# Attention and a four-expert layer on one core: the first second-layer weights summed on another engine, and sums and operands formed at other places

## The chip, the core and the metric

The kernel runs on one core of a Trainium2 chip. The metric is device time in microseconds, the median of several executions; lower is better. TensorE (PE) multiplies matrices, VectorE (DVE), ScalarE (ACT) and GpSimd (POOL) work on tiles, and SyncE (SP) issues the DMA transfers. Each engine takes its instructions in the order in which the program issues them.

## The reference

Attention with a cumulative bias over 32 heads, and then, for each of 2304 tokens, a sum over four experts of two matrix products with a ReLU between them:

```python
attn = softmax(q @ k.T / sqrt(D) + bias)      # 4 x 8 heads, 576 rows, D = 64
x = attn @ v                                  # laid out as 2304 x 512
p = domain_probs / (domain_probs.sum(-1, keepdims=True) + 1e-09)
for e in range(4):
    h = np.maximum(x @ w1[e], 0.0)            # w1[e]: 512 x 1024
    out += p[:, e:e + 1] * (h @ w2[e])        # w2[e]: 1024 x 512
```

## The kernel before

**Stages.** A planner written in the kernel (class Sched) orders the attention, and with it the beginning of expert 0. What remains of expert 0 is emitted by the loop from line 1209 on: a first and a second layer for each group of tokens. Experts 1 to 3 follow in a form of their own, in which the order is written out by hand. The change touches the end of expert 0 and that last part.

**Precision.** Each matrix operand is split in two: a rounded part (hi, on ACT, line 457) and the residue (sub, line 444, mostly on DVE), so a product takes three matmuls per block.

**Items and products.** Experts 1 to 3 are cut into 18 work items: half of an expert's hidden width by a third of the tokens, in the order expert, half, third. Each item has a first and a second layer, and each layer is computed with seven block products in place of eight, on sums of blocks (a Strassen form). One product is twelve matmuls of 128x128 by 128x384: six into each of two PSUM banks (product, line 1262). The program issues the first layer of item 0, then, for each item, the first layer of the next item and after it the second layer of this one.

**Banks.** bA, bB, bC and bM are pairs of PSUM banks. In both layers seven products go to these in the order 1, 6, 5, 7, 2, 4, 3 (first layer, line 1284) and 1, 6, 2, 5, 7, 3, 4 (second layer, line 1382). pass_on (line 1273, "the hand-over") copies one pair into another on ACT: bA to bC after product 1 of the first layer, bC to bB after products 1 and 7 of the second. Product 6 continues in the pair just copied, so it waits for the copy.

**First layer.** keep (line 1297) copies a pair of banks to SBUF on ACT: c12 after product 6, c22 after product 7, in item 0 also c11 and h21. plus (line 1305) adds another pair to it on DVE (line 1307) and then gates it: ReLU times the token's probability (line 1278). c11 is complete after product 2, h21 after product 4, c12 after product 3.

**Second-layer operands.** From c11, c12, c22 and h21 DVE forms s5 = c22 + h21, s7 = c11 - h21, s6 = c11 - s5 and s3 = c12 + s6 (add, line 1055). operand (line 1350) splits c11, c12, c22, s5, s6, s7 and s3 into operands 1, 2, 4, 5, 6, 7 and 3; the residues of 7 and 3 are POOL's, that of 5 is POOL's except in item 0. The tables START, FIRST, EARLY, REST, ALL and LAST (lines 41 to 46) say after which product which of these steps is issued. START belongs to the first layer of item 0. FIRST belongs to the first layer of item 1 and forms operands of item 0. EARLY belongs to the second layers of items 0 to 15 and forms those of the item after; REST belongs to the first layers behind these.

**Second layer.** update (line 1384) adds a pair of banks to acc in SBUF on DVE (line 1390): bC after product 6, bB after 2, bM after 5, bC after 7, bM after 3, bB after 4. Product 3 continues in bM and waits for the update after product 5.

**Weights.** w_steps (line 1125) returns a list: sums (line 1132), which forms sums of the four staged weight blocks, and seven calls of split (line 1145) for the seven weights. side is a list from which both layers take such steps, two after each product in the first layer of item 0. wsteps is its like at the end of expert 0: from the last first-layer group on, the loop takes up to three steps after each group of a layer. Temporary tiles t come from a pool of six; x operands from a pool of seven, each loaded when the product before it in that buffer is done.

The names in the trace have their buffer numbers left out: pb are the banks of bA, bB and bC, mo those of bM, hT_r, xg and hx the operands (hx is operand 3), osb the gate weights.

Of the kernel before, what the change touches and what calls it, by code (L numbers as in the profile page):

```python
# [11 lines left out]
F32 = mybir.dt.float32  # L12
F32R = mybir.dt.float32r
AF = mybir.ActivationFunctionType
ALU = mybir.AluOpType
# [8 lines left out]
P = 128  # L24
NC = 5
TG = 384
# [11 lines left out]
HALVES = [(e, s) for e in range(1, E) for s in range(2)]  # L38
T_PREP = (10.0, 28.0, 47.0)
T_LOAD = 6.0  # L40
START = {7: "4", 4: "1", 3: "s5 s7"}
EARLY = {1: "1", 6: "s5", 2: "2 s7", 5: "s6", 4: "4"}
REST = {1: "6 5", 6: "s3 7", 5: "3"}
ALL = {4: "4", 1: "1", 2: "2", 6: "6", 5: "5", 7: "7", 3: "s3 3"}
LAST = {4: "s5 s7", 3: "s6"}
FIRST = {1: "2 5 s6", 6: "6", 5: "s3 7", 7: "3"}
PRODUCTS = (1, 6, 5, 7, 2, 4, 3)


def rows(m):  # L50
    return (0, 64) if m == 0 else (128 * m - 64, 128 * m + 64)


def t_pe(n):
    return max(n / 2.4 + 13.5, 110)
# [271 lines left out]
def body(ctx, tc, qk, qkv0, vp, s, dp, w1, w1s, w2, w2s, out):  # L327
# [23 lines left out]
    def slot(name, shape, dt, pool=hpool):  # L351

        if late.get(name, (None, None))[0] != dt:
            late[name] = (dt, pool.tile(shape, dt, tag=name, name=f"{name}_{'r' if dt == F32R else 'f'}"))
        return late[name][1]

    def hT(l):
        return slot(f"hT{l}", [P, KF, TG], F32R)
# [84 lines left out]
    def sub(e, out, in0, in1):  # L443
        (nc.gpsimd if e == "POOL" else nc.vector).tensor_tensor(out=out, in0=in0, in1=in1, op=ALU.subtract)  # L444
# [10 lines left out]
    def hi(e, out, in_):  # L455
        if e == "ACT":
            nc.scalar.activation(out, in_, AF.Copy)  # L457
        elif e == "POOL":
            nc.gpsimd.tensor_scalar(out, in_, 1.0, 1.0, op0=ALU.mult, op1=ALU.mult)
        else:  # L460
            nc.vector.tensor_copy(out, in_)
# [183 lines left out]
    for j, (h, ms) in enumerate(VISITS):  # L645
        base = 1000.0 * (j + 1)
        b, hh = divmod(h, NH)
        o = 64 * (hh % 2)
# [71 lines left out]
        for m in ms[1:] if joint else ms:  # L720
            pr = base + PM * m
            a, bb = rows(m)
            n = bb - a
# [181 lines left out]
    for which in (1, 2):  # L905
        for i in range(4):
# [3 lines left out]
            n, lo = 1024 // WH, None  # L910
# [13 lines left out]
    def load_x(tiles, dc):  # L924
        n0, w = tiles[0] * P, len(tiles) * P
        nc.sync.dma_start(out=xgt[:, :, dc, 0:w].bitcast(F32), in_=xw[dc // 2, dc % 2, :, :, n0:n0 + w])
# [3 lines left out]
    def l1_mm(fc, w, t, u0, u1):  # L930
        recent[0] = t
        q, o = fc // 2, 128 * (fc % 2)
        for u in range(u0, u1):
            dc, part = divmod(u, 3)
            wl, l = ((w1h, 0), (w1h, 1), (w1l, 0))[part]
            nc.tensor.matmul(t[:, 0:w], wl[q][:, dc, o:o + P], xgt[:, l, dc, 0:w], start=(u == 0), stop=(u == 3 * KD - 1))  # L936

    def l1_hi(fc, w, t):
        nc.scalar.activation(hT(0)[:, fc, 0:w], t[:, 0:w], AF.Relu)

    def l1_lo(fc, w, t):
        nc.vector.scalar_tensor_tensor(out=hT(1)[:, fc, 0:w], in0=t[:, 0:w], scalar=0.0, in1=hT(0)[:, fc, 0:w].bitcast(F32),
                                       op0=ALU.max, op1=ALU.subtract)
# [70 lines left out]
    mpool = ctx.enter_context(tc.tile_pool(name="moe", bufs=1))  # L1014
    xpool = ctx.enter_context(tc.tile_pool(name="xring", bufs=7))
    tpool = ctx.enter_context(tc.tile_pool(name="temps", bufs=6))
    spool = ctx.enter_context(tc.tile_pool(name="stage", bufs=1))
# [17 lines left out]
    def temp():  # L1035
        return tpool.tile([P, 2, TG], F32, tag="t", name="t")
# [17 lines left out]
    def add(e, out, in0, in1, op):  # L1054
        (nc.gpsimd if e == "POOL" else nc.vector).tensor_tensor(out=out, in0=in0, in1=in1, op=op)  # L1055
# [69 lines left out]
    def w_steps(which, begin=False):  # L1125

        b = stage.pop(which)
        neg = which == 2
        part = w1_part if which == 1 else w2_part
        src = {1: b[0, 0], 2: b[1, 0], 3: b[1, 1], 7: b[0, 1], 4: b[1, 0]}  # L1130

        def sums():
            if begin:
                src[5], src[6], src[4] = (t.rearrange("p a b -> p (a b)") for t in (spool.tile([P, 1, 512], F32, tag="t2", name="t2"), temp(), temp()))
                src[5], src[6], src[4] = (t[:, 0:512] for t in (src[5], src[6], src[4]))
                add("POOL", src[5], b[0, 1], b[0, 0], ALU.subtract)
                add("POOL", src[7], b[1, 1], b[0, 1], ALU.subtract)
                add("POOL", src[6], b[1, 1], src[5], ALU.subtract)
                add("POOL", src[4], b[1, 0], src[6], ALU.subtract)
                return  # L1140
            src[5] = src[6] = spool.tile([P, 1, 512], F32, tag="t2", name="t2")[:, 0]
            add("POOL", src[5], b[0, 1], b[0, 0], ALU.subtract)
            add("POOL", src[7], b[1, 1], b[0, 1], ALU.subtract)

        def split(o, e):
            hi("ACT", part(o, 0), src[o])
            sub(e, part(o, 1), src[o], part(o, 0).bitcast(F32))
            if begin:
                pass
            elif o == 5 and neg:  # L1150
                add("POOL", src[6], src[5], b[1, 1], ALU.subtract)
            elif o == 5:
                add("POOL", src[6], b[1, 1], src[5], ALU.subtract)
            if o == (6 if neg else 2) and not begin:
                add("POOL", src[4], src[4], src[6], ALU.add if neg else ALU.subtract)

        return [sums] + [lambda o=o, e=e: split(o, e) for o, e in (
            tuple((o, "DVE") for o in PRODUCTS) if begin else
            ((5, "POOL"), (1, "POOL"), (2, "POOL"), (6, "POOL"), (4, "POOL"), (7, "DVE"), (3, "DVE")) if which == 1 else
            ((1, "DVE"), (2, "DVE"), (5, "DVE"), (6, "DVE"), (7, "POOL"), (3, "DVE"), (4, "DVE")))]  # L1160

# [7 lines left out]
    def bank(k):  # L1169
        if k in tok:  # L1170
            return tok[k]
        if k not in cur:
            b = nbuf[0] % len(banks)
            cur[k] = 1 - b if b < 2 and banks[b] is recent[0] else b
            nbuf[0] += 1
        return banks[cur[k]]
# [22 lines left out]
    w1_first = []  # L1199
# [8 lines left out]
    wsteps = []  # L1208
    for i, x in enumerate(prog):
        if x[0] == "load":  # L1210
            if x[2].done is None:
                load_x(x[1], x[3])
        elif x[0] == "l1":
            if x[4].done is None:
                l1_mm(x[1], x[2], bank(x[5]), x[3], x[3] + UN)
                spent += UN * t_pe(x[2]) / 1e3
        elif x[0] == "l1e":
            if x[3].done is None:
                l1_hi(x[1], x[2], bank(x[5]))
            if x[4].done is None:  # L1220
                l1_lo(x[1], x[2], bank(x[5]))
        elif x[0] == "l2":
            if x[3].done is None:
                l2_mm(x[1], x[5], bank(x[4]), x[2], x[2] + UN)
                spent += UN * t_pe(x[5]) / 1e3
        else:
            gi, dt = x[1]
            n0, n1 = GROUPS0[gi][0] * P, GROUPS0[gi][-1] * P + P
            if x[2].done is None:
                evict0(gi, dt, bank(x[4]))  # L1230
            else:
                if x[3].done is None:
                    nc.sync.dma_start(out=o_d[dt * P:(dt + 1) * P, n0:n1], in_=tok["osb", x[1]][:, 0:n1 - n0])
                spilled.append((dt, n0, n1))
        if x[0] in ("l1", "l2"):
            while steps and steps[0][0] <= spent:
                steps.pop(0)[3]()
        if i == last_l1:
            wsteps = w1_first
        if i >= last_l1 and wsteps and x[0] in ("l1e", "l2e"):  # L1240
            for _ in range(3):
                if wsteps:
                    wsteps.pop(0)()
# [5 lines left out]
        for b_, u0, u1 in blocks_of(n0, n1):  # L1249
            nc.sync.dma_start(out=acc[dt][b_][:, u0 - TG * b_:u1 - TG * b_], in_=o_d[dt * P:(dt + 1) * P, u0:u1])  # L1250
    bA, bB, bC, bM = ([t[:, 0:TG] for t in ts] for ts in (pb[0:2], pb[2:4], pb[4:6], mo))
    hx = mpool.tile([P, 2, 2, TG], F32R, name="hx")

    def h_part(o, l):
        if o == 3:
            return hx[:, l]
        if o in (6, 7):
            return xgt[:, l, 2 * (o - 6):2 * (o - 6) + 2, :]
        n = (1, 2, 4, 5).index(o)
        return hT(l)[:, 2 * n:2 * n + 2, :]  # L1260
# [21 lines left out]
    side = []  # L1282
# [143 lines left out]
    def next_probs(w_i):  # L1426
        if w_i < len(work):
            n, g = work[w_i]
            load_prob(HALVES[n][0], NP * g, osb2)

    next_probs(0)
    side.extend(w_steps(2))
    tmp = {}
    steps = operands(tmp, e5="DVE")
    first_layer(0, plan(steps, START), tmp)
    next_probs(1)
    for w_i, (n, g) in enumerate(work):
        more = n + 1 < len(HALVES)
        if w_i + 1 < len(work):
# [8 lines left out]
            tmp = {}  # L1448
            at = plan(steps, REST if w_i else FIRST)
            steps = operands(tmp, True, last=w_i + 2 == len(work))  # L1450
# [7 lines left out]
        if g == 2 and more:  # L1458
            w2_next = w_steps(2)
            side.extend(w2_next[:4])  # L1460
            del w2_next[:4]
        second_layer(w_i, n, g, plan(steps, EARLY if w_i + 2 < len(work) else ALL if w_i + 2 == len(work) else {}))
        while side:
# [33 lines left out]
```

## Time and profile before

| | us |
|---|---|
| median of 3 runs | 928.04 (928.01 to 928.5) |
| profiled execution | 928.9 |
| its span | 927.1 |

| engine | busy us | share of the span |
|---|---|---|
| PE | 914.6 | 99% |
| DVE | 676.2 | 73% |
| ACT | 480.0 | 52% |
| POOL | 498.5 | 54% |

The span runs from the first to the last instruction in the profile; the rest of the profiled execution lies around it. Busy time counts an instruction from its start to its end, and matmuls overlap their neighbours. Bracketed times in the timeline are the idle time of that engine just before the row, with the engine, tile and line that released it. x2 means that two like instructions in a row are drawn as one.

### The profile page before, as it was taken

How to read it: one execution, taken by the hardware profiler on the slowest of the kernel's cores; microseconds unless marked ns; L12 is line 12 of the kernel's file. 1: busy time of each engine (PE TensorE's matmuls, PEld its weight loads, DVE VectorE, ACT ScalarE, POOL GpSimd, SP SyncE). 2: the span in 40 equal slices, each digit the busy share in tenths (PEclk: the TensorE clock that was granted, in tenths of full speed). 3: DMA queues.
4: the chain of work that ended last, by engine and by line, in shares of the span. 5: the costliest groups of instructions: out<-in, count | busy, mean ns of one | idle time of the engine just before them, and what ended most of it. 6: DMA issues, size and time to landing. Idle time of an engine off the chain costs nothing.

```text
span 927.1 us, 16473 instructions
## 1 busy us (share of the span) xinstructions
PE 914.6 (99%) x5590; PEld 884.6 (95%) x5590; DVE 676.2 (73%) x1568; ACT 480.0 (52%) x1094; POOL 498.5 (54%) x530
## 2 busy tenths in 40 slices
PE   9999999999999999999999999999999999999998
PEld 6789999899999999988999999999999999999998
DVE  6878788887861121588878787878777878688885
ACT  6898999898960110342444334435343534344342
POOL 4688888787733699120754174536444624471322
PEclk9999999999999999999999999999999999999999
DMA  6788878869526984597775658665786468744703
GB/s 167 188 250 253 225 215 228 239 185 256 168 78 217 327 292 160 164 309 258 255 244 190 217 207 300 207 203 175 273 272 205 160 221 301 243 158 157 269 27 119
DMA packets 131039, 198.85 MB, mean 214 GB/s; under 512 B 11448, under 2 KB 107772, under 8 KB 130956
## 3 DMA queue, kind: packets, MB, share of 16 engines
q1 hardware_dynamic: 130956, 197.81, 66.7%
q8 instruction: 44, 0.72, 0.3%
q14 instruction: 39, 0.32, 0.1%
HBM read 154.85 MB, written 29.05 MB: 198 GB/s over the span
## 4 chain that ended last, share of the span: by engine, by line
PE 84%; DVE 8%; ACT 4%; issue 2%; POOL 1%; DMA 0%; SPq 0%; ACTq 0%; POOLq 0%
PE pb L1267 43%; PE mo L1267 7%; PE mo L950 7%; PE mo L936 6%; PE pv L835 4%; PE pb L936 4%; PE pb L950 3%; PE T L785 3%; PE S L739 3%; PE S L736 1%; DVE acc L1390 1%; DVE hT_r L444 1%; DVE t L1055 1%; PE X L785 1%; ACT a L758 1%
## 5 line engine op out<-in xcount | busy, mean ns | idle before, releaser
L1267 PE MATMUL pb<-x,w1h 128*128 128x384 f32 x1008 | 256.9, 335 | 2.9 <-ACT pb L1275 1.6
L1267 PEld LDWEIGHTS pb<-x,w1h 128*128 128x128 f32 x1008 | 181.0, 188 | 5.9 <-ACT t L1300 2.2
L1267 PE MATMUL pb<-x,w1l 128*128 128x384 f32 x504 | 168.5, 334 | 0.0
L1275 ACT ACTIVATE pb<-pb 128x384 f32<-128x384 f32 x106 | 50.1, 474 | 162.5 <-DVE t L1307 99.5
L444 POOL TENSOR_TENSOR hT_r<-t,hT_r 128x768 fp32r<-128x768 f32 x17 | 31.8, 1873 | 178.6 <-PE pb L1267 143.5
L457 ACT ACTIVATE hT_r<-t 128x768 fp32r<-128x768 f32 x72 | 60.8, 845 | 103.2 <-PE pb L1267 95.1
L1267 PE MATMUL pb<-hT_r,w2h 128*128 128x384 f32 x432 | 109.7, 334 | 0.8 <-DVE t L1278 0.8
L1267 PEld LDWEIGHTS pb<-x,w1l 128*128 128x128 f32 x504 | 94.6, 188 | 0.0
L758 ACT ACTIVATE a<-a,mx 128x576 f32<-128x576 f32 (+4 forms) x136 | 81.0, 597 | 13.3 <-DVE mx L750 10.1
L1390 DVE TENSOR_TENSOR acc<-pb,acc 128x384 f32<-128x384 f32 x144 | 74.7, 551 | 12.4 <-PE pb L1267 9.5
L1267 PEld LDWEIGHTS pb<-hT_r,w2h 128*128 128x128 f32 x432 | 77.9, 188 | 1.1 <-DVE t L1278 1.1
L936 PE MATMUL mo<-xg,w1h 128*128 128x384 f32 (+1 forms) x304 | 78.3, 327 | 0.0
L452 POOL TENSOR_SCALAR a<-a,sm 128x576 f32<-128x576 f32 (+5 forms) x111 | 60.9, 555 | 28.6 <-DVE sm L766 15.0
L444 DVE TENSOR_TENSOR hT_r<-t,hT_r 128x768 fp32r<-128x768 f32 x55 | 57.6, 1049 | 24.0 <-ACT hT_r L457 23.5
L1267 PE MATMUL pb<-xg,w2h 128*128 128x384 f32 x288 | 73.4, 335 | 0.5 <-ACT pb L1275 0.5
L1267 PE MATMUL pb<-hT_r,w2l 128*128 128x384 f32 x216 | 72.2, 334 | 0.0
L1055 DVE TENSOR_TENSOR t<-t 128x768 f32<-128x768 f32 (+1 forms) x40 | 65.0, 1632 | 0.0
L1307 DVE TENSOR_TENSOR t<-pb,t 128x384 f32<-128x384 f32 x74 | 37.8, 552 | 34.6 <-ACT t L1300 22.4
L950 PE MATMUL mo<-hT_r,w2h 128*128 128x256 f32 (+1 forms) x320 | 58.3, 314 | 0.0
L814 DVE TENSOR_TENSOR aTl<-T,aTh 128x256 fp32r<-128x256 f32 (+2 forms) x103 | 51.2, 508 | 4.9 <-ACT aTh L457 3.7
L750 DVE CUSTOM_DVE_ANT_0 a<-S,mask 128x448 f32<-128x448 f32 (+4 forms) x107 | 48.2, 456 | 8.7 <-PE S L736 6.1
L936 PEld LDWEIGHTS mo<-xg,w1h 128*128 128x128 f32 x304 | 52.1, 190 | 1.4 <-issue 0.7
(217 smaller groups left out, 2310.3 us busy)
## 6 DMA issues: line engine op xcount, KB each, us to landing
x<-xs_d SPq DMA_DIRECT2D x68, 768.0 KB
x<-x_d SPq DMA_DIRECT2D x55, 768.0 KB
xs_d<-x SPq DMA_DIRECT2D x12, 768.0 KB
KK<-AB_r SPq DMA_DIRECT2D x24, 288.0 KB
osb<-p_d SPq DMA_DIRECT2D x18, 384.0 KB
xg<-x_d SPq DMA_DIRECT2D x16, 384.0 KB
w1r<-in_w1s_dram SPq DMA_DIRECT2D x6, 1024.0 KB
w2r<-in_w2s_dram SPq DMA_DIRECT2D x6, 1024.0 KB
```

The lines of the kernel that those rows point to most:

```text
L444: (nc.gpsimd if e == "POOL" else nc.vector).tensor_tensor(out=out, in0=in0, in1=in1, op=ALU.subtract)
L452: (nc.gpsimd if e == "POOL" else nc.vector).tensor_scalar(out, in_, scale, 1.0 if bias is None else bias, op0=ALU.mult, op1=ALU.mult if bi ...
L457: nc.scalar.activation(out, in_, AF.Copy)
L750: nc.vector.tensor_tensor_reduce(out=z[0:n, j0:j1], in0=tok["S", (c, pi)][0:n, 0:j1 - j0], in1=mask[0:n, 448 - a + j0:448 - a + j1], scale ...
L758: nc.scalar.activation(z[0:n, 0:bb], z[0:n, 0:bb], AF.Exp, bias=tok["mx", c][0:n, k:k + 1], scale=-1.0, accum_out=tok["sm", c][0:n])
L814: nc.vector.tensor_tensor(out=dst, in0=src, in1=h_.bitcast(F32), op=ALU.subtract)
L936: nc.tensor.matmul(t[:, 0:w], wl[q][:, dc, o:o + P], xgt[:, l, dc, 0:w], start=(u == 0), stop=(u == 3 * KD - 1))
L950: nc.tensor.matmul(t[:, 0:w], wl[fc // 2][:, fc % 2, 128 * dt:128 * dt + 128], ht[:, fc, 0:w], start=(u == 0), stop=(u == 3 * KF - 1))
L1055: (nc.gpsimd if e == "POOL" else nc.vector).tensor_tensor(out=out, in0=in0, in1=in1, op=op)
L1267: nc.tensor.matmul(ts[u], wv[wl][:, k, 128 * u:128 * u + 128], x[xl_][:, k, :], start=start and k == 0 and n == 0, stop=k == 1 and n == 2, ...
L1275: nc.scalar.activation(out[u], in_[u], AF.Copy)
L1390: nc.vector.tensor_tensor(out=d, in0=ts[u], in1=d, op=ALU.add)
```

## The change

The tables START, EARLY and FIRST change. With START and FIRST, s5, s7 and operand 1 of item 0 are formed after product 1 of the next first layer, s6 and operand 6 after product 6, operand 2 and s3 after product 5, operand 5 after product 4, operands 7 and 3 after product 3. With EARLY, s7 follows product 5, operand 2 follows product 7 and s6 follows product 3.

The weights of the first second layer are summed in one step of four subtractions and additions on DVE, as was done for the first-layer weights on POOL, and not with two on POOL at first and two between the splits. This step is issued at the end of expert 0. The sums lie in the memory of hx, which operand 3 takes over later, and the seven residues are all DVE's, in the order 1, 6, 2, 5, 7, 3, 4.

```diff
-START = {7: "4", 4: "1", 3: "s5 s7"}
-EARLY = {1: "1", 6: "s5", 2: "2 s7", 5: "s6", 4: "4"}
+START = {7: "4"}
+EARLY = {1: "1", 6: "s5", 5: "s7", 7: "2", 3: "s6", 4: "4"}
-FIRST = {1: "2 5 s6", 6: "6", 5: "s3 7", 7: "3"}
+FIRST = {1: "s5 s7 1", 6: "s6 6", 5: "2 s3", 4: "5", 3: "7 3"}
...
             if begin:
-                src[5], src[6], src[4] = (t.rearrange("p a b -> p (a b)") for t in (spool.tile([P, 1, 512], F32, tag="t2", name="t2"), temp(), temp()))
-                src[5], src[6], src[4] = (t[:, 0:512] for t in (src[5], src[6], src[4]))
-                add("POOL", src[5], b[0, 1], b[0, 0], ALU.subtract)
-                add("POOL", src[7], b[1, 1], b[0, 1], ALU.subtract)
-                add("POOL", src[6], b[1, 1], src[5], ALU.subtract)
-                add("POOL", src[4], b[1, 0], src[6], ALU.subtract)
+                if which == 1:
+                    ts = (spool.tile([P, 1, 512], F32, tag="t2", name="t2"), temp(), temp())
+                    src[5], src[6], src[4] = (t.rearrange("p a b -> p (a b)")[:, 0:512] for t in ts)
+                else:
+                    t = slot("hx", [P, 2, 2, TG], F32, mpool).rearrange("p a b n -> p (a b n)")
+                    src[5], src[6], src[4] = (t[:, 512 * i:512 * i + 512] for i in range(3))
+                e = "DVE" if neg else "POOL"
+                add(e, src[5], b[0, 1], b[0, 0], ALU.subtract)
+                add(e, src[7], b[1, 1], b[0, 1], ALU.subtract)
+                add(e, src[6], *((src[5], b[1, 1]) if neg else (b[1, 1], src[5])), ALU.subtract)
+                add(e, src[4], b[1, 0], src[6], ALU.add if neg else ALU.subtract)
                 return
...
-            tuple((o, "DVE") for o in PRODUCTS) if begin else
+            tuple((o, "DVE") for o in (PRODUCTS if which == 1 else (1, 6, 2, 5, 7, 3, 4))) if begin else
...
         if i == last_l1:
-            wsteps = w1_first
+            w2_first = w_steps(2, True)
+            wsteps = w1_first + w2_first[0:1]
...
-    hx = mpool.tile([P, 2, 2, TG], F32R, name="hx")
-
     def h_part(o, l):
         if o == 3:
-            return hx[:, l]
+            return slot("hx", [P, 2, 2, TG], F32R, mpool)[:, l]
...
-    side.extend(w_steps(2))
+    side.extend(w2_first[1:])
```

## Rows read from the trace of the kernel before

**Rows 1.** The page's head: the span, and busy time of each engine.
```profile
span 927.1 us, 16473 instructions
...
PE 914.6 (99%) x5590; PEld 884.6 (95%) x5590; DVE 676.2 (73%) x1568; ACT 480.0 (52%) x1094; POOL 498.5 (54%) x530
```

**Rows 2.** Busy us by stretch: length, PE, weight loads, DVE, ACT, POOL, clock, DMA.
```profile
387.60:436.50 48.90, 44.66 (x252) 42.92 (x251) 38.48 (x56) 18.72 (x34) 8.01 (x5) 1.00 0.85 293
436.50:525.00 88.50, 88.26 (x506) 87.24 (x506) 70.86 (x105) 37.29 (x65) 41.19 (x23) 1.00 0.66 225
```

**Rows 3.** Timeline of PE: start, length, operation, count, idle time before and releaser.
```profile
387.61 0.52 PE L1267 MATMUL pb<-x,w1h 128*128 128x384 f32 x2
...
404.10 0.34 PE L1267 MATMUL pb<-x,w1l 128*128 128x384 f32 x1
406.04 0.61 PE L1267 MATMUL pb<-x,w1h 128*128 128x384 f32 x2 [1.60 <-ACT pb L1275]
...
424.42 0.62 PE L1267 MATMUL pb<-xg,w2h 128*128 128x384 f32 x2 [0.54 <-ACT pb L1275]
...
462.13 0.61 PE L1267 MATMUL mo<-hx,w2h 128*128 128x384 f32 x2
...
491.81 0.62 PE L1267 MATMUL mo<-hx,w2h 128*128 128x384 f32 x2 [0.24 <-DVE acc L1390]
...
550.60 0.61 PE L1267 MATMUL mo<-hx,w2h 128*128 128x384 f32 x2
```

**Rows 4.** Waits of the weight loads from 376 on: total us, times, longest us.
```profile
PEld mo L1267 <- DVE acc L1390: 4.4, 10, 0.6
...
PEld pb L1267 <- ACT t L1300: 2.2, 6, 0.7
```

**Rows 5.** Timeline of ACT, 395 to 425.
```profile
395.71 0.64 ACT L457 ACTIVATE w2h<-t 128x512 fp32r<-128x512 f32 x1 [2.21 <-POOL t L1055]
...
396.77 0.86 ACT L1300 ACTIVATE t<-pb 128x384 f32<-128x384 f32 x2
...
404.77 0.84 ACT L457 ACTIVATE hT_r<-t 128x768 fp32r<-128x768 f32 x1 [2.35 <-DVE t L1278]
405.52 0.85 ACT L1275 ACTIVATE pb<-pb 128x384 f32<-128x384 f32 x2
...
423.89 0.86 ACT L1275 ACTIVATE pb<-pb 128x384 f32<-128x384 f32 x2 [5.60 <-PE pb L1267]
```

**Rows 6.** Timeline of DVE, 390 to 462.
```profile
390.94 0.69 DVE L444 TENSOR_TENSOR w2l<-w2r,w2h 128x512 fp32r<-128x512 f32 x1 [2.70 <-ACT w2h L457]
...
397.66 1.02 DVE L1307 TENSOR_TENSOR t<-pb,t 128x384 f32<-128x384 f32 x2
...
408.45 1.96 DVE L1055 TENSOR_TENSOR t<-t 128x384 f32<-128x384 f32 x4
410.32 1.82 DVE L444 TENSOR_TENSOR hT_r<-t,hT_r 128x768 fp32r<-128x768 f32 x2
412.06 0.95 DVE L1055 TENSOR_TENSOR t<-t 128x768 f32<-128x768 f32 x1
...
418.38 2.63 DVE L1278 SCALAR_TENSOR_TENSOR t<-t,osb 128x768 f32<-128x768 f32 x1
...
447.11 2.07 DVE L1278 SCALAR_TENSOR_TENSOR t<-t,osb 128x768 f32<-128x768 f32 x1
...
458.89 1.78 DVE L444 TENSOR_TENSOR hT_r<-t,hT_r 128x768 fp32r<-128x768 f32 x1
460.60 1.00 DVE L1055 TENSOR_TENSOR t<-t,pb 128x384 f32<-128x384 f32 x2
461.53 1.01 DVE L1390 TENSOR_TENSOR acc<-mo,acc 128x384 f32<-128x384 f32 x2
```

**Rows 7.** Timeline of POOL: residues of operand 3.
```profile
418.37 1.83 POOL L444 TENSOR_TENSOR hx<-t,hx 128x768 fp32r<-128x768 f32 x1 [1.77 <-ACT hx L457]
...
448.32 2.57 POOL L444 TENSOR_TENSOR hx<-t,hx 128x768 fp32r<-128x768 f32 x1
```

## The prediction, made before the change was run

> **What bounds the kernel now.** I read the page's head first: PE is busy 914.6 of 927.1 us [rows 1]. So almost all of the time is matmuls, and this change removes none of them: it can only win back PE's idle time. The busy time by stretch says where that is: 4.24 us between 387.6 and 436.5, and about 0.25 in each later stretch of three items [rows 2]. "Idle" is too small a figure, because matmuls overlap; their starts are a better ruler. From 387.61 to 404.10 PE starts 96 matmuls without a stop [rows 3]: 16.49 / 95 = 0.1736 us each, 2.083 us for a product of twelve. By that ruler the second product of the first second layer, fifteen products after 387.61, should start at 387.61 + 15 x 2.083 = 418.86; it starts at 424.42 [rows 3]: **5.56 us lost** in five stops. Product 3 of the second layer of item 1 starts at 462.13 and that of item 4 at 550.60 [rows 3]; 42 products are 87.49 us, the distance is 88.47: **0.98 us lost in every three items**. The weight loads' waits name two causes: ten waits for the update of acc, 4.4 us, and six for a copy on ACT, 2.2 us, of which one of 0.7 belongs to the first stretch [rows 4]. Per three items that is 0.88 against 0.30, so about 0.74 of the 0.98 is the update's. Five such periods: 3.7 us.
>
> Then I read ACT and DVE at those places, as both take their instructions in program order. ACT: the rounding of operand 1 waits 2.35 us for DVE's gate, and the hand-over of bA behind it runs only at 405.52 [rows 5], though product 1 had ended at 404.4; PE stands 1.60 for it [rows 3]. Before that, a weight rounding stands 2.21 us for a sum on POOL, and the copy of c22 runs at 396.77 behind it [rows 5]. DVE never catches up after that: it works without a gap through s5, s7, the residues of operands 2 and 5, s6 and the rest, and the hand-over at 423.89 that releases PE at 424.42 is the end of this one chain [rows 3, 5, 6].
>
> **The change, part by part.** *Weight sums on DVE, early.* Four 128x512 sums come in after the first layer of expert 0, behind the second eviction. No row shows this operation on DVE; the nearest, same shape and two SBUF inputs, takes 0.69 [rows 6], so 2.8 us at most, from about 383 to 386. Below nothing it can't be for DVE, but POOL loses four operations. The cover: DVE has nothing to do but two evictions of mo until 390.94, where it had waited 2.70 us for ACT [rows 6]; mo is written again only in the second layer, 35 us later. So 0. The gain: no weight rounding waits for POOL. The seventh weight's residue moves from POOL to DVE, 0.61 to 0.69, into those same waits. The copy of c22 then runs when product 7 is done: that product starts at 387.61 + 3 x 2.083 = 393.86, its last matmul ends at 396.11, the second half of the copy runs from 396.19 to 396.67, and DVE takes up c22 at 396.70 instead of 397.66 [rows 6].
>
> *Operands of the first item later.* I walk DVE on from 396.70 in the new order. Steps: 1.05 for an addition in two halves (1.02, and 0.03 from its releaser's end), 0.87 for a 128x768 operation with another behind it (two take 1.82, one takes 0.95), 0.61 for a 128x512 one, 1.87 for s5 and s7 together [rows 6]. c22 added and gated to 398.71; ACT rounds operand 4 (0.84 and two releases [rows 5]), its residue starts at 399.70; then w4, c11 added, two gates, c12 added, its gate: 0.87 + 0.61 + 1.05 + 1.74 + 1.05 + 0.87 = 6.19, to 405.89. s5, s7, residue 1, s6: 1.87 + 0.87 + 0.95, to 409.6. ACT rounds operand 6, residue at 410.5; 6, 2 and s3: 2.61, to 413.1; c22 of item 1 added, to 414.2. The PE dates, if nothing stops it: item 1 begins at 402.19, its products start every 2.083, product 3 at 414.69, the second layer at 416.78. Hence: the hand-over of bA has only ready work ahead of it on ACT, 1.60 saved; the copy of c12 stands behind operand 1 alone, whose gate ended long before; c22 is added 0.5 us before product 3 wants bB. **Four of the five stops go.**
>
> The fifth grows. POOL's residue of operand 7 starts when ACT has rounded it. ACT's queue there is: 6 (from 409.63), 2, the copy of c22, 5, 7, at 0.75 each (404.77 to 405.52 [rows 5]), so 7 is rounded by 413.5. The gate of c22 at 414.2 has two SBUF inputs and meets this residue. The trace shows what that does: the same gate took 2.63 instead of 0.95 at 418.38, and ended 0.82 after POOL's operation begun at 418.37 [rows 6, 7]. So here it ends at 413.52 + 1.83 + 0.82 = 416.2. Behind it: c11 (0.93), h21 (0.93), the residue of operand 5, now ahead of it (0.87), c12 added (1.01): 419.9. ACT hands bC over to bB from 419.97 and PE follows 0.53 after the start of that copy, as at 423.89 and 424.42 [rows 3, 5]: **420.50 instead of 424.42, 3.92 us gained**; a stop of 1.6 stays. Bounds: without the block, 1.2 us sooner; with a second one at operand 5, up to 1.7 later (a POOL residue's 1.83 less 0.1). I take the middle, as the walk hits the one and just passes the other.
>
> The Trainium skill (SBUF — State Buffer, section "SBUF: two separate sides") says that whichever of a DVE operation with two SBUF inputs and a GpSimd one starts first holds the shared port for its whole instruction; the rows agree (2.63). It states no turns for the one that waits. In the trace DVE gets in between two POOL operations: at 447.11 a gate waits 2.07 and ends at 449.18, and the POOL operation queued from 448.32 takes 2.57 instead of 1.83 [rows 6, 7]. By a reading without turns the gate would wait for both residues; that is a rival below.
>
> *DMA.* No transfer is added. The load of the next gate weights follows the gate of c12 on the SP queue, about 2.5 us earlier now, and with it the first-layer weights and item 2's operands behind it. Before, it had at most 418.38 - 408.45 = 9.9 us until its use [rows 6]; now it has 8.2. Bounds 0 to 1.7; 0 taken, since nothing waited for it. Item 1's operands are each used 12.5 us after the product that frees their buffer; product 1 already had no more, and did not wait. 0.
>
> *Second layers.* Product 3 accumulates in bM and must wait until the update after product 5 has read it. Item 2's operand 2 and s7 stand ahead of that update on DVE: residue 2 from 458.89 (1.78, POOL in its way), s7 from 460.60, the update only from 461.53, PE at 462.13 [rows 3, 6]. Moved away, the update follows product 5 directly: that starts at 462.0 - 2 x 2.083 = 457.8, is finished by 460.1, the update by 460.7, over 1 us ahead of product 3. The same holds for the longer stop at 491.81 [rows 3]. **All ten stops go, 3.7 us.** What is late next: s7 stands ahead of the update after product 7, and bC is wanted again 4 us later by the hand-over; residue 2 ahead of the update after product 3, bM is wanted a layer later; s6 ahead of the last update, bB is wanted by product 5 of the next layer, 4.2 us after its start. Each delays by 0.9 to 1.8 us. On ACT operand 2's rounding stands behind the hand-over, and ACT has room. The 0.24 per period of the copy on ACT stays.
>
> **Sum.** 3.92 + 3.7 = 7.6 us. Span 927.1 - 7.6 = 919.5; the profiled execution took 928.9, 1.8 around its span, so 921.3; the median of the runs shown, 928.04, lies 0.86 below that execution: **920.4**.
>
> **The rivals.**
> - *No turn for DVE at the port* (the skill's rule without turns): the gate also waits for the residue of operand 3, 1.83 more: 922.2. Against it: 449.18. 0.10.
> - *No block*, POOL comes after the gate: 919.2. 0.10.
> - *The second-layer stops return*, for instance residue 2 blocked by POOL twice, or the update after product 7 too late: up to 3.7 lost, 924.1. The slack of over 1 us speaks against it. 0.10.
> - *Slower:* s6 is now formed almost last; its rounding for operand 6 stands on ACT ahead of the copy of c12 that product 7 of the next first layer waits for. That copy tolerates a rounding start 4.2 us into the layer (product 7 at 6.25, less 1.5 for two roundings and 0.5 for half a copy). s6 would end 0.1 to 1 us into it; blocked by POOL once more 1.7 later, still in time. From 4.2 on each us is lost in 16 items; at 4.8 the change is worth 7.6 - 16 x 0.6 = -2 us: 930. 0.04.
> - *It does little:* the walk's slack is not there and the same length of chain returns in other places, 927 to 928. 0.04.
>
> **How the numbers follow.** The forecast has 0.62. 0.2% here is 1.9 us, about what a measurement of this kernel can tell from no change. Faster holds the forecast and the first three rivals, 0.92; same 0.04; slower 0.04. The range takes in the forecast with its bounds, the missing block and the missing turn: 918.9 to 923.0.
>
> **What would show it.** Right: the hand-over of bA before 404.5; ACT's weight roundings without a wait for POOL; product 6 of the first second layer near 420.5, with one stop of 1.6 ahead of it; no weight load waiting for acc; three items in 87.7 us. Wrong: a wait of PE for a copy of c12 in many items, new waits for bB or bC in second layers, or several stops ahead of 418.9.

## The result, and the profile after

| | before | changed |
|---|---|---|
| median | 928.02 us | 919.95 us (919.86 to 920.34) |
| profiled execution | 928.9 | 919.93 |
| its span | 927.1 | 918.2 |

The ratio is 0.9913, with a 95% interval of 0.9896 to 0.9931: 8.1 us less. The forecast was 920.4.

The head of the page after, to be held against [rows 1]:

```profile
span 918.2 us, 16474 instructions
...
PE 910.0 (99%) x5590; PEld 883.8 (96%) x5590; DVE 669.6 (73%) x1573; ACT 478.8 (52%) x1094; POOL 486.5 (53%) x525
```

The same 5590 matmuls; five operations moved from POOL to DVE. Busy time by stretch of the changed kernel, in the columns of [rows 2] (the stretches are the same parts of the work, a little earlier and shorter):

```profile
387.60:432.60 45.00, 43.60 (x251) 43.03 (x250) 36.19 (x57) 18.93 (x35) 4.36 (x2) 1.00 0.92 319
432.60:520.10 87.50, 87.50 (x505) 87.12 (x504) 69.70 (x104) 36.92 (x66) 40.19 (x23) 1.00 0.68 227
```

PE is idle 1.40 us in the first stretch instead of 4.24, and in the stretch of three items not at all by this count. The timeline of PE in the changed kernel gives the exact loss, as [rows 3] did:

```profile
386.41 0.51 PE L1271 MATMUL pb<-x,w1h 128*128 128x384 f32 x2
...
417.66 0.34 PE L1271 MATMUL pb<-hT_r,w2l 128*128 128x384 f32 x1
419.40 0.62 PE L1271 MATMUL pb<-xg,w2h 128*128 128x384 f32 x2 [1.40 <-ACT pb L1279]
...
456.97 0.51 PE L1271 MATMUL mo<-hx_r,w2h 128*128 128x384 f32 x2
...
544.67 0.51 PE L1271 MATMUL mo<-hx_r,w2h 128*128 128x384 f32 x2
```

From the first product of item 0 to product 6 of the first second layer it is now 419.40 - 386.41 = 32.99 us; before it was 424.42 - 387.61 = 36.81 [rows 3]. **3.82 us gained there.** From product 3 of item 1 to that of item 4 it is 87.70 instead of 88.47 [rows 3]: **0.77 in three items, 3.9 us in five such periods.** The weight loads wait for acc no more; of the six waits for a copy on ACT the five of the later items are left (columns as in [rows 4]):

```profile
PEld pb L1271 <- ACT pb L1279: 2.1, 3, 1.7
PEld pb L1271 <- ACT t L1304: 1.5, 5, 0.3
PEld pb L1271 <- DVE t L1282: 0.3, 1, 0.3
```

The spans differ by 8.9, which is 1.2 more than these two sums, and 1.2 is also by how much the part of experts 1 to 3 begins earlier. The 1.2 is there before the changed weight sums start (the same group of sixteen matmuls starts at 378.97 before and at 377.77 after), so it comes from what stands ahead of the change, attention and the most of expert 0. The busy time of 164 to 168 and of 168 to 172, of the kernel before and then of the changed kernel, shows where it is from:

```profile
164.00:168.00 4.00, 2.96 (x20) 2.17 (x19) 3.20 (x11) 2.85 (x9) 2.71 (x7) 1.00 0.95 294
168.00:172.00 4.00, 4.00 (x19) 3.72 (x18) 2.58 (x10) 3.58 (x9) 3.21 (x4) 0.58 0.97 234
...
164.00:168.00 4.00, 2.94 (x20) 2.15 (x19) 3.19 (x11) 2.85 (x9) 2.69 (x7) 1.00 0.91 262
168.00:172.00 4.00, 4.00 (x28) 3.83 (x27) 2.92 (x11) 3.93 (x9) 3.21 (x4) 1.00 0.96 245
```

In the profiled execution of the kernel before, TensorE's granted clock was 0.58 of 2.4 GHz from 168 to 172, so mostly its lower level of 1.2 GHz, and 19 matmuls ran where 28 run after. PE was busy throughout these 4 us, and for 2.96 of the 4 us before them; in the changed kernel it was busy for 2.94 of those 4 us, and the clock stayed. That is chance of one execution and no part of the change. Without it the traces differ by 7.7. The spans on record agree: 25 executions of the kernel before ran beside the experiments, the 19 with a mean clock of 0.999 or 1.000 have a median span of 925.9, the six others 927.1 to 927.4, and the changed kernel's four lie at 918.1 to 918.6. The medians differ by 8.1; the other 0.4 is not in the traces and stays open.

### The profile page after: what moved, and what is told of

Its sections match the earlier page's. It is cut to its first block, busy times and chain, and to the rows that moved or that the text cites. A ratio compares the mean times of both kernels' runs of the same rounds, so it can differ in the third digit from the quotient of the medians.

```text
span 918.2 us, 16474 instructions
## 1 busy us (share of the span) xinstructions
PE 910.0 (99%) x5590; PEld 883.8 (96%) x5590; DVE 669.6 (73%) x1573; ACT 478.8 (52%) x1094; POOL 486.5 (53%) x525
## 4 chain that ended last, share of the span: by engine, by line
PE 92%; DVE 4%; ACT 2%; issue 1%; POOL 0%; ACTq 0%; POOLq 0%; DVEq 0%
PE pb L1271 47%; PE mo L1271 8%; PE mo L936 7%; PE mo L950 7%; PE pv L835 5%; PE pb L936 4%; PE T L785 3%; PE pb L950 3%; PE S L739 3%; PE S L736 1%; PE X L785 1%; ACT a L758 1%; DVE t L1282 1%; DVE t L1311 0%; ACT aTh L457 0%
## 5 line engine op out<-in xcount | busy, mean ns | idle before, releaser
L444 POOL TENSOR_TENSOR xg<-t,xg 128x768 fp32r<-128x768 f32 x18 | 41.1, 2282 | 44.0 <-ACT xg L457 44.0
L1055 DVE TENSOR_TENSOR t<-t 128x768 f32<-128x768 f32 (+1 forms) x40 | 61.2, 1535 | 0.1
L1271 PEld LDWEIGHTS pb<-xg,w2h 128*128 128x128 f32 x288 | 51.8, 188 | 2.1 <-ACT pb L1279 2.1
```

Of the source, the lines that this page charges most:

```text
L1271: nc.tensor.matmul(ts[u], wv[wl][:, k, 128 * u:128 * u + 128], x[xl_][:, k, :], start=start and k == 0 and n == 0, stop=k == 1 and n == 2, ...
```

## Experiments

Each diff is against the changed kernel. The medians of the kernel before, run beside them, were 927.84, 928.01 and 927.92.

### The old order in second layers

```diff
-EARLY = {1: "1", 6: "s5", 5: "s7", 7: "2", 3: "s6", 4: "4"}
+EARLY = {1: "1", 6: "s5", 2: "2 s7", 5: "s6", 4: "4"}
```

> The changed kernel with the old table EARLY alone. My theory (the update after product 5 was late because operand 2 and s7 stood ahead of it on DVE): the ten waits for acc come back, three items take 88.47 us again instead of 87.69, five times 0.78 = 3.9 us more, 923.8; the first stretch stays as it is (product 6 of the first second layer near 419.4 of the span). Rival (the stops in second layers were an after-effect of DVE's backlog from the first stretch): they stay away, 920.0.

Measured: 924.16 us, 4.2 more than the changed kernel. The waits of the weight loads are back, the timeline of DVE shows the old queue, and the first stretch has kept its single stop:

```profile
PEld mo L1271 <- DVE acc L1394: 4.3, 10, 0.6
...
420.63 0.61 PE L1271 MATMUL pb<-xg,w2h 128*128 128x384 f32 x2 [1.38 <-ACT pb L1279]
...
455.12 1.77 DVE L444 TENSOR_TENSOR hT_r<-t,hT_r 128x768 fp32r<-128x768 f32 x1
456.82 1.01 DVE L1055 TENSOR_TENSOR t<-t,pb 128x384 f32<-128x384 f32 x2
457.75 1.01 DVE L1394 TENSOR_TENSOR acc<-mo,acc 128x384 f32<-128x384 f32 x2
```

Operand 2's residue, s7, and only then the update that product 3 waits for, as in [rows 6]. Product 6 of the first second layer starts 32.99 us after this kernel's first product (387.64), as in the changed kernel. The rival, an after-effect of the first stretch, falls.

### Operand 2 or s7 alone in its old place

```diff
-EARLY = {1: "1", 6: "s5", 5: "s7", 7: "2", 3: "s6", 4: "4"}
+EARLY = {1: "1", 6: "s5", 2: "2", 5: "s7", 3: "s6", 4: "4"}
```

> The changed kernel with operand 2 back after product 2 in EARLY; s7 and s6 stay late. My theory (the update after product 5 has 1.4 us of slack once both are gone, and either of the two alone, 0.9 to 1.8 us on DVE, is just covered): no or few waits for acc, 920.0 to 920.6. Rival (operand 2 alone brings the waits back): 923.8.

```diff
-EARLY = {1: "1", 6: "s5", 5: "s7", 7: "2", 3: "s6", 4: "4"}
+EARLY = {1: "1", 6: "s5", 2: "s7", 7: "2", 3: "s6", 4: "4"}
```

> The changed kernel with s7 back after product 2 in EARLY; operand 2 and s6 stay late. My theory (as for operand 2; s7 takes 0.93 us and does not meet POOL): no waits for acc, 920.0. Rival (s7 alone brings them back): 923.8.

Measured: 919.81 and 920.00, both as the changed kernel, and no wait for acc in either. With operand 2 back, DVE in the second layer of item 1:

```profile
453.79 1.77 DVE L444 TENSOR_TENSOR hT_r<-t,hT_r 128x768 fp32r<-128x768 f32 x1
455.48 1.01 DVE L1394 TENSOR_TENSOR acc<-mo,acc 128x384 f32<-128x384 f32 x2
```

The update runs 1.4 us later than in the changed kernel, where its first half starts at 454.05; that half is done by 456.04, and product 3 starts without a wait at 456.87. So it took both steps to make the stop, and moving one would have done.

### The old places of the first item's operands

```diff
-START = {7: "4"}
+START = {7: "4", 4: "1", 3: "s5 s7"}
-FIRST = {1: "s5 s7 1", 6: "s6 6", 5: "2 s3", 4: "5", 3: "7 3"}
+FIRST = {1: "2 5 s6", 6: "6", 5: "s3 7", 7: "3"}
```

> The changed kernel with the old tables START and FIRST alone; the weight sums stay early and on DVE. My theory (one DVE chain decides, and both edits shorten it): the copy of c22 stays early, so operand 1 is rounded by 404 and the first stop all but vanishes by the sums alone; but operands 2 and 5 and the two POOL residues meet s3 and the gate as before, and the chain ends about 1.6 us sooner than in the kernel before and 2.3 later than in the changed one: 922.2. Rival (the early sums are worth nothing by themselves, the tables do it all): 923.8.

Measured: 922.23. ACT and then PE:

```profile
402.04 0.85 ACT L457 ACTIVATE hT_r<-t 128x768 fp32r<-128x768 f32 x1 [2.27 <-DVE t L1282]
402.79 0.94 ACT L1279 ACTIVATE pb<-pb 128x384 f32<-128x384 f32 x2
...
421.69 0.61 PE L1271 MATMUL pb<-xg,w2h 128*128 128x384 f32 x2 [0.53 <-ACT pb L1279]
```

Operand 1's rounding still waits for DVE, but the wait ends in time, since the copy of c22 is no longer late; of the first stop little is left. Product 6 starts 421.69 - 386.41 = 35.28 us after the first product: 1.53 sooner than before, 2.29 later than in the changed kernel. So the early sums, with the order and the engine of their residues, are worth 1.5 without the two tables.

### The old weight sums

```diff
-            w2_first = w_steps(2, True)
-            wsteps = w1_first + w2_first[0:1]
+            wsteps = w1_first
...
-    side.extend(w2_first[1:])
+    side.extend(w_steps(2))
```

> The changed kernel with the second-layer weight sums as they were, two on POOL in the first layer of item 0 and two between the splits; all three tables new. My theory: the copy of c22 waits again behind two weight roundings (0.96 us), and two weight residues instead of one stand ahead of c11 on DVE (0.61): the chain is 1.6 us longer and ends so much later, 921.5. Rival (the sums are hidden, the tables do it all): 920.0.

Measured: 921.35. A weight rounding waits for POOL again, and product 6 starts at 420.81, 34.50 us after this kernel's first product (386.31), 1.51 later than in the changed kernel:

```profile
394.42 0.64 ACT L457 ACTIVATE w2h<-t 128x512 fp32r<-128x512 f32 x1 [2.21 <-POOL t L1055]
...
420.81 0.61 PE L1270 MATMUL pb<-xg,w2h 128*128 128x384 f32 x2 [1.38 <-ACT pb L1278]
```

The tables alone are worth 3.82 - 1.51 = 2.3, the sums alone 1.5, both together 3.82. They add up, as they should if both shorten one chain.

### The stop that was left: operand 5, then operands 7 and 3

```diff
-FIRST = {1: "s5 s7 1", 6: "s6 6", 5: "2 s3", 4: "5", 3: "7 3"}
+FIRST = {1: "s5 s7 1", 6: "s6 6", 5: "2 s3", 3: "5 7 3"}
```

> The changed kernel with operand 5 of item 0 issued after product 3 of the first layer of item 1, so that its residue no longer stands ahead of the addition of c12 on DVE. My theory (the stop of 1.6 us that is left at product 6 of the first second layer is the end of DVE's chain): 0.87 us shorter, 919.1, a stop of about 0.7 left. Rival (POOL's residues at the shared port set the end, so the place of this one does not matter): 919.9.

Measured: 918.90, and PE's idle time ahead of product 6 falls from 1.40 to 0.52.

```diff
-FIRST = {1: "s5 s7 1", 6: "s6 6", 5: "2 s3", 4: "5", 3: "7 3"}
+FIRST = {1: "s5 s7 1", 6: "s6 6", 5: "2 s3", 3: "5"}
+FIRST2 = {1: "7 3"}
...
+            late_steps = plan(steps, FIRST2) if not w_i else {}
...
+            at2 = {o: late_steps.get(o, []) + at2.get(o, []) for o in set(at2) | set(late_steps)}
```

FIRST2 belongs to the second layer of item 0; its steps stand ahead of EARLY's.

> As op5_late, and operands 7 and 3 of item 0 issued after product 1 of the first second layer, behind the hand-over, so that POOL's residues no longer meet the gate of c22 at the shared port. My theory (the gate is lengthened by POOL's residue, 1.88 instead of 0.96, and this lies on the chain): the gate takes 0.96, the stop of 0.8 left in op5_late goes, 918.1. Rival (the chain is set elsewhere, or the residues of 7 and 3 now come too late for products 7 and 3): 918.9 or more.

Measured: 918.32. The gate of c22 in this kernel, and POOL's two residues, now after it:

```profile
413.11 0.96 DVE L1283 SCALAR_TENSOR_TENSOR t<-t,osb 128x768 f32<-128x768 f32 x1
...
419.01 1.85 POOL L445 TENSOR_TENSOR xg<-t,xg 128x768 fp32r<-128x768 f32 x1 [50.35 <-ACT xg L458]
420.82 2.56 POOL L445 TENSOR_TENSOR hx_r<-t,hx_r 128x768 fp32r<-128x768 f32 x1
```

The gate takes 0.96 and PE has no idle time left in this stretch. By the medians that is 0.6 less, where 0.8 was expected. Both terms of the chain are shown.

### s6 last

```diff
-EARLY = {1: "1", 6: "s5", 5: "s7", 7: "2", 3: "s6", 4: "4"}
+EARLY = {1: "1", 6: "s5", 5: "s7", 7: "2", 4: "4 s6"}
```

> The changed kernel with s6 in EARLY issued after product 4, behind operand 4's residue, the last place in the second layer. My theory of the slack (operand 6's rounding may start 4.2 us into the next first layer before the copy of c12 is late for product 7; s6 now ends within 1 us of its beginning, here about 2): no change, 920.0. Rival (the slack is smaller, the slower case of the forecast): up to 1 us for each of 16 items, 921 to 936.

Measured: 922.05, 2.1 us more. **My expectation fell.** First DVE with s6, ACT, where operand 6's rounding now waits for it, and PE ahead of product 4, then the waits of the weight loads over the expert part, and last s6 and the same rounding in the changed kernel:

```profile
492.10 0.95 DVE L1055 TENSOR_TENSOR t<-t 128x768 f32<-128x768 f32 x1
...
493.14 0.85 ACT L457 ACTIVATE xg<-t 128x768 fp32r<-128x768 f32 x1 [0.25 <-DVE t L1055]
...
501.03 0.62 PE L1271 MATMUL pb<-x,w1h 128*128 128x384 f32 x2 [0.32 <-ACT t L1304]
...
PEld pb L1271 <- ACT t L1304: 3.2, 5, 0.7
...
489.73 0.94 DVE L1055 TENSOR_TENSOR t<-t 128x768 f32<-128x768 f32 x1
...
492.96 0.84 ACT L457 ACTIVATE xg<-t 128x768 fp32r<-128x768 f32 x1
```

The five waits for a copy on ACT grew from 1.5 to 3.2 us. It is the copy of c22, ahead of product 4, and not that of c12, whose slack I had worked out. By PE's starts the five stops grew by 0.33 each, 1.6 in all, and one at product 6 of the second layer of item 16 grew by 0.6.

### Operand 3 later

```diff
-REST = {1: "6 5", 6: "s3 7", 5: "3"}
+REST = {1: "6 5", 6: "s3 7", 7: "3"}
```

> The changed kernel with operand 3 issued after product 7 and not after product 5 in the first layers of items 2 to 17. My theory of the five stops that are left, one every three items (the copy of c22 stands on ACT behind operand 3's rounding, which waits for s3 on DVE): they go, five times 0.26 = 1.3, 918.6. Rival (the weight roundings of that layer hold the copy, not operand 3): 919.9.

Measured: 919.56, only 0.4 less. The five waits are gone as expected, 1.3 us, so the rival falls, but a new stop takes the place of most of it. PE is shown at product 6 of the second layer of item 16, where it stops, then DVE and POOL near the end of item 17's first layer, before it, and last the same gate in the changed kernel:

```profile
887.50 0.62 PE L1271 MATMUL pb<-xg,w2h 128*128 128x384 f32 x2 [1.00 <-ACT pb L1279]
...
879.79 2.44 DVE L1282 SCALAR_TENSOR_TENSOR t<-t,osb 128x768 f32<-128x768 f32 x1
...
879.57 1.84 POOL L444 TENSOR_TENSOR hx_r<-t,hx_r 128x768 fp32r<-128x768 f32 x1 [1.14 <-issue]
...
880.54 1.27 DVE L1282 SCALAR_TENSOR_TENSOR t<-t,osb 128x768 f32<-128x768 f32 x1
```

In that layer alone s5 and s7 are formed too (table LAST), and POOL's residue of operand 3, begun only 0.2 us ahead of the gate, now keeps it waiting for nearly its whole length: 2.44 instead of 1.27. That the stop comes of this was not shown until the last run below.

Together with the late operands 5, 7 and 3 of item 0:

```diff
-REST = {1: "6 5", 6: "s3 7", 5: "3"}
+REST = {1: "6 5", 6: "s3 7", 7: "3"}
-FIRST = {1: "s5 s7 1", 6: "s6 6", 5: "2 s3", 4: "5", 3: "7 3"}
+FIRST = {1: "s5 s7 1", 6: "s6 6", 5: "2 s3", 3: "5"}
+FIRST2 = {1: "7 3"}
...
```

> op73_late and rest3 together. My theory (the stop of the first stretch and the five small ones have separate causes): the gains add, 919.95 - 1.8 - 1.3 = 916.9. Rival (they share slack on DVE or POOL): about 918.

Measured: 918.03, with the same new stop. The last kernel keeps operand 3's old place in the first layer of item 17 alone (FIRST and FIRST2 are those of the run before):

```diff
 REST = {1: "6 5", 6: "s3 7", 5: "3"}
+REST7 = {1: "6 5", 6: "s3 7", 7: "3"}
...
-            at = plan(steps, REST if w_i else FIRST)
+            at = plan(steps, (REST if w_i + 2 == len(work) else REST7) if w_i else FIRST)
+            late_steps = plan(steps, FIRST2) if not w_i else {}
...
```

> The kernel of the run best, with operand 3's old place in the first layer of item 17 alone. My theory (the stop of 1.2 us that appeared in that item's second layer comes from the late residue of operand 3, which meets the gate of c22 on POOL while s5 and s7 stand in the same chain there): it goes, and the gains add as first worked out, 916.9. Rival (it comes from the five stops being gone, not from operand 3's place in item 17): 918.0.

Measured: **916.57 us, ratio to the kernel before 0.988 (0.9865 to 0.9895)**, 3.4 less than the changed kernel. Busy time by stretch: PE is busy without a gap in the first stretch and in the three items, and of the waits of the weight loads over the expert part only the last line is left.

```profile
386.00:432.00 46.00, 46.00 (x268) 45.85 (x267) 36.71 (x59) 19.92 (x36) 4.37 (x2) 1.00 0.92 312
520.00:607.00 87.00, 87.00 (x504) 86.93 (x503) 72.41 (x104) 37.01 (x65) 40.22 (x23) 1.00 0.68 228
...
PEld pb L1273 <- ACT pb L1281: 0.4, 2, 0.2
```

Two waits of 0.2 are all, so the stop of 887.50 came from operand 3's place in the first layer of item 17.

## Why the prediction was right, point by point

**Where the loss was.** Right: the loss sat in PE's stops, 5.56 us in the first stretch and about a microsecond in every three items, and the gains of 3.82 and 3.9 us are all that the change moved in the traces.

**Weight sums on DVE.** Right in cost and gain. No row of before had shown the operation; here are the four sums and the evictions around them, then the copy of c22 on ACT:

```profile
381.80 0.69 DVE L1055 TENSOR_TENSOR hx_f<-w2r 128x512 f32<-128x512 f32 x1
382.51 0.69 DVE L1055 TENSOR_TENSOR w2r<-w2r 128x512 f32<-128x512 f32 x1
383.12 0.69 DVE L1055 TENSOR_TENSOR hx_f<-hx_f,w2r 128x512 f32<-128x512 f32 x1
383.84 0.69 DVE L1055 TENSOR_TENSOR hx_f<-w2r,hx_f 128x512 f32<-128x512 f32 x1
384.45 0.42 DVE L1196 TENSOR_TENSOR acc<-mo,osb 128x256 f32<-128x256 f32 x1
...
394.94 0.49 ACT L1304 ACTIVATE t<-pb 128x384 f32<-128x384 f32 x1 [0.49 <-PE pb L1271]
```

They take 2.73 us from first start to last end, against a bound of 2.8, in DVE's free time. The second half of the copy of c22 waits for PE alone, not for weights. By the two trials with old places this was worth 1.5 of the 3.82 us.

**The chain of the first item.** Right in its steps. One reading of the kernel before was not exact: DVE did not work without a gap there, it waited 0.92 us at 413.93 for the rounding of operand 6; the walk had this wait in it. The walk gave 418.86 as PE's own date and 420.50 as the end of the chain; the part of experts 1 to 3 begins 1.20 earlier in this trace, so 419.30 is to be compared with 419.40. Four of the five stops went; all that is left ahead of the second layer is a hesitation of 0.2 at 415.64, where the walk had nothing to spare. The fifth grew as foreseen; here is the end of the chain, DVE and then POOL, to be held against [rows 6, 7]:

```profile
412.19 1.02 DVE L1311 TENSOR_TENSOR t<-pb,t 128x384 f32<-128x384 f32 x2
413.24 1.88 DVE L1282 SCALAR_TENSOR_TENSOR t<-t,osb 128x768 f32<-128x768 f32 x1
415.04 1.01 DVE L1282 SCALAR_TENSOR_TENSOR t<-pb,osb 128x384 f32<-128x384 f32 x2
415.97 1.02 DVE L1282 SCALAR_TENSOR_TENSOR pb<-pb,osb 128x384 f32<-128x384 f32 x2
416.90 0.94 DVE L444 TENSOR_TENSOR hT_r<-t,hT_r 128x768 fp32r<-128x768 f32 x1
417.77 1.01 DVE L1311 TENSOR_TENSOR t<-pb,t 128x384 f32<-128x384 f32 x2
...
412.45 1.85 POOL L444 TENSOR_TENSOR xg<-t,xg 128x768 fp32r<-128x768 f32 x1 [43.49 <-ACT xg L457]
414.26 2.55 POOL L444 TENSOR_TENSOR hx_r<-t,hx_r 128x768 fp32r<-128x768 f32 x1
```

The gate, 1.88 long, ends at 415.12, 0.82 after POOL's first residue; the second residue stretches to 2.55. DVE gets its turn between the two, and the rival without a turn falls: it would have put product 6 at 421.2. The rival without a block falls with the gate's 1.88. The middle between the bounds held by a narrow margin, as the walk had said: the residue of operand 5 starts at 416.90, and POOL's second residue had ended at 416.81.

The Trainium skill (SBUF — State Buffer, section "SBUF: two separate sides") describes the exclusive lock that this shows, and the trace agrees, 1.88 here against 0.96 without POOL beside it. What happens when a third operation is queued comes from the trace alone.

**DMA.** Taken as 0, and no wait for a transfer shows among PE's waits in this part, nor any idle time of DVE ahead of the gate at 413.24.

**Second layers.** Right in mechanism, a little small in size: 3.7 forecast, 3.9 measured. The step that was mis-sized is the split of the 0.98 between two causes by the weight loads' waits, which gave the update 0.74; by the products' starts it was 0.77. The stated slack, over 1 us, agrees with the runs that put one step back: 1.4 us later, the update still came in time.

**The rival on the slower side** had the right place and the wrong wait. s6 does decide late work: formed about 2.5 us later against PE's products (at 492.10, in the changed kernel at 489.73, in traces 0.16 apart there), it made operand 6's rounding 0.3 us later and cost 2.1 us in all; but through s3, operand 3 and the copy of c22, which had no slack in every third item, and not through the copy of c12. In the changed kernel s6 was early enough: it ends at 490.67, and operand 6's rounding starts at 492.96 behind the hand-over.

**The sum.** 7.6 forecast, 7.7 by the traces, 8.1 by the medians. The sum came down from the profiled execution to the median by 0.86 without a reason given; the dip of the clock in that one execution, 1.2 us, is enough for it.

## What to carry to other kernels

Where one engine is busy 99%, measure its stops by the distance between starts of equal work, not by idle time: here 4.24 us of idle time hid 5.56 of loss. Then walk each in-order queue from the first late instruction to the one that releases the bound engine; an instruction that waits there delays all that stands behind it, and moving the ones not yet needed behind the one that is needed was worth just their length here (0.87 us for the residue of operand 5), up to the slack. Before a step is moved later, look at every consumer's slack, the next but one too: behind operand 6's rounding the copy of c12 could still wait, and the copy of c22, two steps on, could not.

## What the runs showed of the hardware

An operation on VectorE with two SBUF inputs that met one on GpSimd waited for its end, and a second GpSimd operation queued behind then waited for VectorE's: 1.88 us for 0.96 and 2.55 for 1.85, alternately. Operations on VectorE that read PSUM ran at their usual 1.01 to 1.02 beside the same GpSimd operations. And TensorE's granted clock fell to 0.58 over 4 us in the middle of attention in one execution, and stayed at 1.00 in another of the same instructions, with PE busy for 2.96 and 2.94 of the 4 us before.
